# Attention outputs moved to the middle of a slot, their copies to its end, in a top-k attention and mixture-of-experts kernel

## Chip, cores and metric

The kernel runs on one core of a Trainium2 chip. The metric is the device time of one execution in microseconds (us), lower is better. The core's engines are called by the short names of the profile: PE (TensorE: matmuls and transposes; PEld is its weight load), DVE (VectorE), ACT (ScalarE), POOL (GpSimd) and SP (SyncE, which issues transfers).

## What is computed

Two blocks follow each other. The first is attention with a top-k mask: 8 batches, 8 heads, 576 tokens, head size 64; every row of scores keeps its 32 largest values. The second is a mixture of experts without dropping: 4608 tokens of 512 numbers, 8 experts with a hidden size of 1024, and each token goes to the one expert with the highest logit.

```python
scores = scale * np.matmul(q, k.transpose(0, 1, 3, 2))
kth = np.partition(scores, -top_k, axis=-1)[..., -top_k:-top_k + 1]
scores = np.where(scores >= kth, scores, -1000000000.0)
attn = np.exp(scores - np.max(scores, axis=-1, keepdims=True))
attn = attn / (np.sum(attn, axis=-1, keepdims=True) + 1e-09)
attn_out = np.matmul(attn, v)
x = attn_out.transpose(0, 2, 1, 3).reshape(B * S, H * D)
...
logits = x @ w_gate
expert_idx = np.argmax(logits, axis=1)
...
h = np.maximum(x_sorted[lo:hi] @ w1[e], 0.0)
y_sorted[lo:hi] = h @ w2[e]
...
return (gate_w[:, None] * y)
```

## The kernel before

The attention works on *units*: a unit is one batch and one pair of heads, so there are four units to a batch. Two units are worked off together, an even and an odd one. For each such pair the function groups gives nine *slots*; a slot is two tiles of 128 queries by 576 keys. Slots 0 to 3 of the nine are the four full tiles of the even unit, slot 4 has the 64 remaining queries of both units, and slots 5 to 8 are the full tiles of the odd unit. Eight batches with two pairs each make 144 slots. They are numbered through from 0 here, so slot i has the place i modulo 9.

All engines' queues for this stage are written out by hand in loop: the order in which the Python code calls the engines is the order of each engine's queue. One turn of the loop is one slot, and its work is spread over neighbouring turns:

- multiply makes the products of queries and keys (tile sc, L304, on PE) four slots ahead. They go to a pool of score banks in PSUM.
- scores copies them out (tile s, L311, on ACT) three slots ahead.
- search (L379, L390, L356, L320, L321, L327, L335, on DVE) finds the 32 largest values of each row in four rounds of eight. Each round takes one maximum per tile (L379), and the first three also strike the found values out (L390). The fold of the next slot's scores (L320, L321) stands ahead of the rounds, and fold_on (L327, and L335 for the tile hl) stands behind round two or ahead of round four. hl can also be made on POOL (L332, L333).
- When the search ends, ACT takes the threshold (tile low, L401), makes depths (L417) from it, POOL subtracts (less, L426), and ACT takes the exponentials (weights, L434), which leave their sums in z.
- transposed turns the exponentials of the slot before: PE transposes into wTm (L445, two banks), ACT copies them to wT (L452, or L450 in the slots with remaining queries), then PE transposes the rest to wTl (L461, L459) and ACT copies it to wTt (L469, L467).

The banks wTm, wTl, po and px come from one pool with the tag "t" that has two buffers, which are handed out in turn. A matmul into a bank waits until the copy out of the bank's last user is done.

When a unit's last full tile has been opened (place 3 for an even unit, place 8 for an odd one), loop starts ending for it. ending is a generator: it yields the name of the place in the loop at which it wants to go on, and at_place lets those go on that wait for the place it names. Through outputs it makes, step by step, po (weights times values, L482, two halves), its copies oT (L484, ACT), then px (L493, PE, turned back and multiplied by the gate), and the copies xl (L500, ACT). Between the two halves it calls divisors: ACT writes the sums plus epsilon to rz (L504, and L506, L507 or L509), and DVE takes the reciprocal (L511). The reciprocal is put on the list aside; tick takes one step from that list after each maximum and each strike of round three and four of a search, unless the slot is marked heavy. After that, logits (L519 to L524) and rows (L533) run on POOL and use xl and the reciprocal. The last unit of a batch then chooses the experts, ranks the tokens (ranks, places) and scatters them to the rows of their experts.

Expert blocks fill PE's time between. A block has 16 pieces (a piece of the first half is L979, one of the second L996), and pieces runs as many as a credit allows: a rate that the function level gives, times a share that depends on the slot's place. evacuate lets ACT copy out what a block has finished (xTs L870, hT L984, y L1005). In the last batch KEEP pieces are kept back, so that PE has work while the last unit's rows are sorted; after that the remaining blocks run.

The places of one turn of loop stand in this order before the change: the search (with "rows" beside it on POOL where the slot is heavy), "small", depths, less, "pool" (from slot 66 on also "relu" and "rows"), scores, "relu" (up to slot 65), evacuate, "turn", the wTm step, pieces, the wTl step, pieces, weights, the wTt copy, evacuate, multiply, the start of ending, "products", "weights", pieces.

Of the kernel before, what the change touches and what calls it, by code (L numbers as in the profile page):

```python
# [44 lines left out]
def kernel(  # L45
# [47 lines left out]
    nc = tc.nc  # L93
    B, U, P, _ = qk.shape
# [5 lines left out]
    NC = 4  # L100
    SM = NC * P
    ST = S - SM
    KC = NC + 1
# [4 lines left out]
    NT = 2 * NC + 1  # L108
# [25 lines left out]
    k = SimpleNamespace()  # L134
# [76 lines left out]
    for n in range(2):  # L211
        t = const.tile([P, S if n else KC * P], F32, name=f"oT{n}")
# [3 lines left out]
        t = const.tile([P, NT + 1], F32, name=f"rz{n}")  # L216
# [254 lines left out]
    def outputs(n, x):  # L471

        odd = n.u % 2
        oT = oT_of[odd]
        for j in range(2):
            q = slice(j * HF + (0 if odd else ST), (j + 1) * HF + (0 if odd else ST))
            po = bank("po")
            for c in range(KC):
                for h in range(2):
                    r = slice(h * D, (h + 1) * D)  # L480
                    rhs = wT[:, c, h, q] if c < NC else wTt[:, q]
                    nc.tensor.matmul(po[r, 0:HF], n.v[:, c, r], rhs, start=(c == 0), stop=(c == KC - 1))  # L482
            yield
            nc.scalar.copy(oT[:, j * HF:(j + 1) * HF], po[:, 0:HF])  # L484
            yield
        starts = [t * P + (ST if odd else 0) for t in range(NC)] + [0 if odd else SM]
        xw = P + lw
        n.xl = k.small.tile([P, KC, xw], F32, name="xl", bufs=1)
        put = []
        for t0, t1 in ((0, KC - 2), (KC - 2, KC)):  # L490
            px = bank("px")
            for t in range(t0, t1):
                nc.tensor.matmul(  # L493
                    px[:, (t - t0) * xw:(t - t0 + 1) * xw], oT[:, starts[t]:starts[t] + P],
                    turn[:, n.u // 2, odd * lw:odd * lw + xw], start=True, stop=True,
                )
            put.append((n.xl[:, t0:t1, :], px[:, 0:(t1 - t0) * xw].rearrange("p (t w) -> p t w", w=xw)))
        yield
        for to, px in put:
            nc.scalar.copy(to, px)  # L500

    def divisors(n):
        rz = rz_of[n.u % 2]
# [378 lines left out]
    def evacuate(upto=None):  # L882

        while due and (upto is None or upto in [kind for kind, _ in due]):
            due.pop(0)[1]()
# [127 lines left out]
            evacuate()  # L1013

    PIECES = 2 * FT
    FIRST = 13
    ARRIVED = 13
    AHEAD = 3
    QUIET = 66
    ON_CHIP = 3  # L1020
# [3 lines left out]
    with fast:  # L1024
# [86 lines left out]
        def ending(b, u):  # L1111

            nonlocal left
            n = unit[b * U + u]
# [22 lines left out]
            next(out_steps)  # L1137
            yield "relu"
            next(out_steps, None)
            yield "rows"  # L1140
            through(div)
            logits(n, lg)
# [7 lines left out]
            yield "turn"  # L1150
            through(r.steps)
            nc.scalar.activation(lg, lg, AF.Exp)
            yield "products"
            ranks(r)
            yield "small"
            steps = places(r, x)
            aside.append(steps)
            yield "relu"
            nc.scalar.copy(run, r.run)
            if b:  # L1160
                nc.scalar.activation(blocks, r.run, AF.Copy, scale=1.0 / P, bias=UNDER)
# [45 lines left out]
        late = []  # L1207

        def at_place(name):
            for end in list(late):  # L1210
                if end[1] == name:
                    end[1] = next(end[0], None)
                    if end[1] is None:
                        late.remove(end)
# [18 lines left out]
        def loop():  # L1233
# [16 lines left out]
            for i, (b, g) in enumerate(work):  # L1250
                tiles = tiles_of(i)
                u, tile = g[0]
                if tile == 0 and u % 2 == 0:
                    open_unit(tiles[0][0])
                if tails(tiles):
                    open_unit(tiles[1][0])

                loose = 0 < i < QUIET
                k.heavy = loose and "rows" in [place for _, place in late]
                soon = loose and (k.heavy or not k.crowded)  # L1260
                then = behind = beside = lambda: None
                if i + 1 < len(work):
                    def behind():
                        f_of[i + 1] = fold(s_of[i + 1])

                    then = lambda: fold_on(f_of[i + 1], soon and not k.heavy)
                    if i:
                        behind()
                        behind = lambda: None
                if k.heavy:  # L1270
                    beside = lambda: at_place("rows")
                held = k.heavy and k.crowded
                low, nbias, doubts = search(tiles, s_of[i], f_of.pop(i), then, soon, behind, beside)
                k.crowded, k.heavy = held, False
                at_place("small")
                w_of[i] = depths(s_of[i], low)
                less(s_of.pop(i), w_of[i])
                doubts()
                at_place("pool")
                if not loose:  # L1280
                    at_place("relu")
                    at_place("rows")
                put_stores()
                scatter(1)
                at = i % per_batch
                if at == FIRST and b:
                    rate = level(b) * PIECES / (U * NT)
                credit += rate * len(g)
                room = left
                if b == B - 1 and at >= ARRIVED:  # L1290
                    room -= KEEP
                    credit = room / (len(work) - i)
                share = {0: 0.5, 1: 1.2, 2: 1.6, 3: 0.5, 2 * NC: 1.4}[tile]
                now = max(0, min(int(credit * share + 0.5), room))
                credit -= now
                clock = i
                if i + AHEAD < len(work):
                    s_of[i + AHEAD], steps = scores(got_of.pop(i + AHEAD))
                    for step in steps:
                        step()  # L1300
                if loose:
                    at_place("relu")
                evacuate()
                at_place("turn")
                turns = turning(i - 1) if i else iter(())
                next(turns, None)
                part = min(BETWEEN, now - now // 2)
                rest = pieces(part)
                next(turns, None)
                rest = pieces(now - now // 2 - part + rest)  # L1310
                weights(tiles, w_of[i], nbias)
                next(turns, None)
                evacuate()
                if i + AHEAD + 1 < len(work):
                    multiply(i + AHEAD + 1)
                if tile == NC - 1:
                    end = ending(b, u)
                    late.append([end, next(end)])
                at_place("products")
                at_place("weights")  # L1320
                credit = min(credit + pieces(now // 2 + rest), 6 * rate)

            k.between = True
            for _ in turning(len(work) - 1):
                pieces(1)
            assert len(late) == 1
            clock = None
            for place in late[0][0]:
# [145 lines left out]
```

## Time and profile before

The time is the median of three runs. The profile is of one further execution.

| what | value |
| --- | --- |
| median of 3 runs | 1282.63 us (1281.47 to 1285.32) |
| the profiled execution: its own time | 1284.61 us |
| the profiled execution: its span | 1283.0 us |
| PE busy | 1176.1 us, 92% of the span |
| DVE busy | 1058.8 us, 83% |
| ACT busy | 933.3 us, 73% |
| POOL busy | 732.0 us, 57% |
| mean granted clock of TensorE | 0.967 |
| oT copies (L484) on ACT | 64, mean 399 ns |
| xl copies (L500) on ACT | 64, mean 463 ns |
| divisors (L504) on ACT | 32, mean 211 ns |
| reciprocals (L511) on DVE | 32, mean 207 ns |
| hl on DVE (L335) and on POOL (L332) | 107 and 37 |

The page is read from the slices of the span: they show which engine is full in which stage, and the shares over the whole span hide that the attention and the blocks behind it have different limits. A group of instructions is a line of the kernel, an engine, an operation and a tile, with the idle time of the engine just before it and what ended that idle time. Matmuls are pipelined and their ends modelled, so PE's busy time is a rough measure.

### The profile page before, as it was taken

How to read it: one execution, taken by the hardware profiler on the slowest of the kernel's cores; microseconds unless marked ns; L12 is line 12 of the kernel's file. 1: busy time of each engine (PE TensorE's matmuls, PEld its weight loads, DVE VectorE, ACT ScalarE, POOL GpSimd, SP SyncE). 2: the span in 40 equal slices, each digit the busy share in tenths (PEclk: the TensorE clock that was granted, in tenths of full speed). 3: DMA queues.
4: the chain of work that ended last, by engine and by line, in shares of the span. 5: the costliest groups of instructions: out<-in, count | busy, mean ns of one | idle time of the engine just before them, and what ended most of it. 6: DMA issues, size and time to landing. Idle time of an engine off the chain costs nothing. (4 is left out here: it accounts for less than half of the span.)

```text
span 1283.0 us, 24461 instructions
## 1 busy us (share of the span) xinstructions
PE 1176.1 (92%) x7574; PEld 823.6 (64%) x7574; DVE 1058.8 (83%) x4608; ACT 933.3 (73%) x2136; POOL 732.0 (57%) x884
## 2 busy tenths in 40 slices
PE   6767767898899999999999999999999999999998
PEld 3444444665566566667666666666666667789975
DVE  8999999999999999999999999999999965000000
ACT  4888887988799888888788888888888872112121
POOL 4777777786678665658555855676557743101010
PEclk9888788999899999999999999999999999999999
DMA  5001113741474147533946464547555548996582
GB/s 153 31 30 31 31 39 126 263 157 39 146 251 162 39 150 283 182 135 98 332 142 218 163 224 153 189 146 264 178 178 202 172 149 285 353 358 235 215 301 83
DMA packets 98701, 220.81 MB, mean 172 GB/s; under 512 B 5309, under 2 KB 26301, under 8 KB 98560
## 3 DMA queue, kind: packets, MB, share of 16 engines
q1 hardware_dynamic: 91360, 198.87, 44.5%
q0 software_dynamic: 6384, 19.97, 4.2%
q8 instruction: 61, 1.00, 0.3%
q14 instruction: 80, 0.66, 0.2%
q10 hardware_dynamic: 816, 0.31, 0.1%
HBM read 195.75 MB, written 24.04 MB: 171 GB/s over the span
## 5 line engine op out<-in xcount | busy, mean ns | idle before, releaser
L426 POOL TENSOR_TENSOR w<-s,w 128x576 f32<-128x576 f32 x288 | 409.2, 1441 | 317.5 <-ACT w L417 317.4
L979 PE MATMUL ph<-xTs,w 128*128 128x128 f32 x2112 | 263.0, 278 | 2.6 <-ACT xTs L870 2.6
L979 PEld LDWEIGHTS ph<-xTs,w 128*128 128x128 f32 x2112 | 251.3, 194 | 21.1 <-issue 17.6
L996 PE MATMUL py<-w,hT 128*128 128x512 f32 x528 | 248.7, 600 | 1.9 <-ACT hT L984 1.6
L434 ACT ACTIVATE w<-w,nbias 128x576 f32<-128x576 f32 x288 | 223.0, 785 | 2.3 <-POOL w L426 1.4
L445 PE MATMUL wTm<-turn,w 128*128 128x128 f32 x1152 | 173.9, 291 | 52.7 <-ACT oT L484 29.1
L417 ACT ACTIVATE w<-s,low 128x576 f32<-128x576 f32 x288 | 207.7, 768 | 4.7
L304 PE MATMUL sc<-qkb 64*128 64x288 f32 (+1 forms) x1280 | 200.7, 465 | 7.8 <-DMA qkb<-in_qk_dram 4.0
L445 PEld LDWEIGHTS wTm<-turn,w 128*128 128x128 f32 x1152 | 135.1, 148 | 111.6 <-ACT oT L484 35.5
L311 ACT COPY s<-sc 128x576 f32<-128x576 f32 x288 | 168.0, 634 | 11.9 <-PE sc L304 11.8
L379 DVE MAX8 tops<-scr 128x8 f32<-128x168 f32 x576 | 169.5, 328 | 0.0
L452 ACT COPY wT<-wTm 128x512 f32<-128x512 f32 x256 | 140.7, 596 | 37.8 <-PE wTm L445 37.2
L379 DVE MAX8 tops<-few 128x8 f32<-128x144 f32 (+1 forms) x576 | 154.9, 314 | 0.0
L304 PEld LDWEIGHTS sc<-qkb 64*128 64x128 f32 (+1 forms) x1280 | 107.1, 190 | 71.5 <-issue 35.2
L996 PEld LDWEIGHTS py<-w,hT 128*128 128x128 f32 x528 | 92.0, 191 | 86.5 <-issue 83.0
L482 PE MATMUL po<-wT,vb 128*64 128x288 f32 x1024 | 143.8, 425 | 0.0
L888 POOL DMA_INDIRECT out_dram<-y,xg x37 | 38.9, 1052 | 161.3 <-ACT y L1005 82.0
L356 DVE MAX8 few<-l 128x8 f32<-128x288 f32 x288 | 129.8, 451 | 0.0
L320 DVE TENSOR_TENSOR h<-s 128x576 f32<-128x576 f32 (+1 forms) x145 | 111.7, 770 | 3.9 <-ACT s L311 3.6
L321 DVE TENSOR_TENSOR l<-s 128x576 f32<-128x576 f32 (+1 forms) x145 | 114.3, 788 | 0.0
L482 PEld LDWEIGHTS po<-wT,vb 128*64 128x64 f32 x1024 | 70.1, 141 | 68.9 <-issue 17.4
L356 DVE MAX8 few<-hl 128x8 f32<-128x72 f32 x576 | 102.3, 221 | 0.0
(205 smaller groups left out, 1596.7 us busy)
## 6 DMA issues: line engine op xcount, KB each, us to landing
w<-in_moe_w_dram SPq DMA_DIRECT2D x74, 2048.0 KB, 9.2
qkb<-in_qk_dram SPq DMA_DIRECT2D x31, 608.0 KB, 3.8
vb<-in_v_dram SPq DMA_DIRECT2D x32, 320.0 KB, 3.2
xg<-x_rows SPq DMA_DIRECT2D x37, 257.0 KB, 9.1
x_rows<-blank SPq DMA_DIRECT2D x13, 257.0 KB, 7.9
x_rows<-blank POOLq DMA_DIRECT2D x4, 257.0 KB, 9.8
x_rows<-x,posi POOLq DMA_INDIRECT x40, 3.2
out_dram<-y,xg POOLq DMA_INDIRECT x37, 3.9
```

What stands on the lines that cost most here:

```text
L304: nc.tensor.matmul(ps[rows, j, 0:HF], n.q[d, cols], n.k[d, keys], start=True, stop=True)
L311: lambda m=m, ps=ps: nc.scalar.copy(s[:, m, :, :], ps[:, :, 0:HF]) for m, ps in enumerate(got)
L356: nc.vector.max(out=f.few[:, m, QF + 8 * j:QF + 8 * j + 8], in_=away)
L379: nc.vector.max(out=tops[:, m, r * 8:(r + 1) * 8], in_=src[m])
L417: nc.scalar.activation(w[:, m, :], s[:, m, :, :].rearrange("p j k -> p (j k)"), AF.Relu, scale=-STEEP, bias=low[:, m:m + 1],)
L426: k.last_pool = in_turn(nc.gpsimd.tensor_tensor(w[:, m, :], s[:, m, :, :].rearrange("p j k -> p (j k)"), w[:, m, :], op=ALU.subtract)).ins
L434: nc.scalar.activation(w[:, m, :], w[:, m, :], AF.Exp, scale=scale, bias=nbias[:, m:m + 1], accum_out=n.z[:, c:c + 1])
L445: nc.tensor.transpose(pm[:, c * P:(c + 1) * P], w[:, m, first:first + P], ident)
L452: nc.scalar.copy(wT[:, :, m, q], pm4)
L482: nc.tensor.matmul(po[r, 0:HF], n.v[:, c, r], rhs, start=(c == 0), stop=(c == KC - 1))
L979: nc.tensor.matmul(ph[:, f, :], n.w1[:, 0, dt, fc * P:(fc + 1) * P], n.xT[:, dt, :], start=(dt == 0), stop=(dt == DT - 1),)
L996: nc.tensor.matmul(py, hT[:, f, :], n.w2[:, 0, f, :], start=(f == 0), stop=(f == FT - 1))
```

## The change

In outputs the copies of px follow each half of px rather than both, with a step in between, so px takes two slots. In ending the second half of px and its copy are steps of their own ("products", "relu"), and rows come after a further place. In loop the place "products" moves from the end of the turn to its middle, between the wTm and the wTl step, and multiply moves along, behind it; the place "relu", at which the copies and the divisors are issued, moves from behind the score copies to behind the wTt copy. New places "ranks" and "early" keep the ranking and the copy of its counts where "products" and "relu" were. Rows run beside the search in all slots. FIRST and ARRIVED, the places at which a new batch's blocks enter the credit, go from 13 to 14, and the shares of pieces are given for each of the nine places.

```diff
     def outputs(n, x):
...
-        put = []
         for t0, t1 in ((0, KC - 2), (KC - 2, KC)):
             px = bank("px")
...
-            put.append((n.xl[:, t0:t1, :], px[:, 0:(t1 - t0) * xw].rearrange("p (t w) -> p t w", w=xw)))
-        yield
-        for to, px in put:
-            nc.scalar.copy(to, px)
+            yield
+            nc.scalar.copy(n.xl[:, t0:t1, :], px[:, 0:(t1 - t0) * xw].rearrange("p (t w) -> p t w", w=xw))
+            if t1 < KC:
+                yield
...
-    FIRST = 13
-    ARRIVED = 13
+    FIRST = 14
+    ARRIVED = 14
+    SHARES = (0.5, 0.5, 1.05, 1.6, 0.5, 1.6, 0.55, 1.1, 1.6)
...
             next(out_steps, None)
+            yield "products"
+            next(out_steps)
+            yield "relu"
+            next(out_steps, None)
+            yield "weights"
             yield "rows"
...
-            yield "products"
+            yield "ranks"
             ranks(r)
...
-            yield "relu"
+            yield "early"
             nc.scalar.copy(run, r.run)
...
-                k.heavy = loose and "rows" in [place for _, place in late]
-                soon = loose and (k.heavy or not k.crowded)
+                k.heavy = "rows" in [place for _, place in late]
+                soon = k.heavy or loose and not k.crowded
...
                 at_place("pool")
-                if not loose:
-                    at_place("relu")
-                    at_place("rows")
                 put_stores()
...
-                share = {0: 0.5, 1: 1.2, 2: 1.6, 3: 0.5, 2 * NC: 1.4}[tile]
+                share = SHARES[i % NT]
...
-                if loose:
-                    at_place("relu")
+                at_place("early")
                 evacuate()
                 at_place("turn")
                 turns = turning(i - 1) if i else iter(())
                 next(turns, None)
                 part = min(BETWEEN, now - now // 2)
                 rest = pieces(part)
+                at_place("products")
+                if i + AHEAD + 1 < len(work):
+                    multiply(i + AHEAD + 1)
                 next(turns, None)
                 rest = pieces(now - now // 2 - part + rest)
                 weights(tiles, w_of[i], nbias)
                 next(turns, None)
+                at_place("relu")
                 evacuate()
-                if i + AHEAD + 1 < len(work):
-                    multiply(i + AHEAD + 1)
                 if tile == NC - 1:
                     end = ending(b, u)
                     late.append([end, next(end)])
-                at_place("products")
+                at_place("ranks")
                 at_place("weights")
...
             for _ in turning(len(work) - 1):
                 pieces(1)
+            at_place("rows")
```

## The prediction

> **What bounds the kernel now.** I read the page's slices (part 2) first, then the busy time by stages, the waits of PE, and last the timeline of one slot. Each digit of the slices is a tenth of busy time in 32 us:
>
> ```profile
> PE   6767767898899999999999999999999999999998
> DVE  8999999999999999999999999999999965000000
> PEclk9888788999899999999999999999999999999999
> ```
>
> VectorE stands at 9 from the second slice until the attention ends, near 1047 us; after that PE alone is full. The busy time by stages (columns: stage, length, then busy us of PE, PE's weight loads, DVE, ACT, POOL, then clock and DMA) sharpens it:
>
> ```profile
> 20.00:100.00 80.00, 57.45 (x320) 35.20 (x320) 80.00 (x353) 67.82 (x156) 62.33 (x77) 0.85 0.10 33
> 100.00:500.00 400.00, 339.66 (x2185) 224.58 (x2185) 399.76 (x1762) 342.25 (x795) 291.48 (x351) 0.93 0.38 133
> 600.00:1000.00 400.00, 393.04 (x2640) 269.94 (x2642) 398.08 (x1697) 341.36 (x791) 247.36 (x291) 1.00 0.56 197
> ```
>
> VectorE is never idle: 399.76 of 400 us, then 398.08. So each of the 144 slots lasts as long as its VectorE work (6.55 us with hl on GpSimd, 6.9 to 7.1 without, more where sums for the routing ride along), and what makes VectorE wait lengthens the attention by as much. Behind it about 235 us of expert blocks follow on PE (1047 to 1283), a fixed number of them. PE's waits from 500 to 1047 us, and then from 20 to 500 us:
>
> ```profile
> PE wTl L461 <- ACT wT L452: 5.2, 11, 1.1
> ...
> PE wTm L445 <- ACT xl L500: 0.9, 1, 0.9
> ```
>
> ```profile
> PE wTm L445 <- ACT oT L484: 29.1, 21, 3.5
> PE wTl L461 <- ACT wT L452: 21.0, 20, 3.1
> PE wTm L445 <- ACT xl L500: 16.4, 6, 3.4
> ```
>
> PE's waits for the oT and xl copies, 45.5 us, lie before 500 us, where PE has room and VectorE sets the pace. Removing them there buys nothing by itself.
>
> One slot in which an odd unit makes its divisors (timeline, start and length in us):
>
> ```profile
> 77.46 0.20 ACT L401 ACTIVATE low<-tops 128x2 f32<-128x2 f32 x1 [1.16 <-DVE tops L379]
> ...
> 80.09 0.41 ACT L484 COPY oT<-po 128x288 f32<-128x288 f32 x1
> ...
> 80.38 0.23 ACT L504 ACTIVATE rz<-z 128x9 f32<-128x9 f32 x1
> 80.49 0.20 ACT L506 ACTIVATE rz<-z 64x1 f32<-64x1 f32 x1
> ...
> 80.72 0.20 ACT L507 ACTIVATE rz<-z 64x1 f32<-64x1 f32 x1
> 80.82 1.04 ACT L452 COPY wT<-wTm 128x512 f32<-128x512 f32 x2
> ...
> 82.57 0.21 DVE L511 RECIPROCAL rz<-rz 128x10 f32<-128x10 f32 x1
> ...
> 83.42 0.24 ACT L469 COPY wTt<-wTl 128x128 f32<-128x128 f32 x1
> ```
>
> The search of slot 9 ends when low starts. VectorE goes straight into search 10, and 5.11 us later reaches the reciprocal of this unit's divisors, which ScalarE wrote 1.65 us before. That margin is what the change spends.
>
> **What the Trainium skill says.** *PSUM — Partial Sum Buffer*, "Engine vs sequencer instructions": the queues of ScalarE, VectorE and GpSimd are strict FIFO, and matmuls start and end in program order. The timeline agrees: the search went on only behind the reciprocal. *TensorE: Matmul & The Clock Gate*, "What's actually happening": the array's clock is throttled unless recent activity releases it. The stages agree: clock 0.85 where PE is 72% busy, 1.00 where it is 98%. *SBUF — State Buffer*, "Who interferes with whom": a VectorE operation with two SBUF inputs contends with GpSimd's reads. Moving rows (L533, 1253 to 1804 ns) may thus cost VectorE some tenths; I take 0.
>
> **The change, part by part.** Times below count from low.
>
> *Divisors.* They go from behind the score copies to the end of ScalarE's queue for the slot, behind the exponentials, wTt and oT. In the built program's order the reciprocal stays where it was, in the next search behind the first of the two maxima of round three (due at 5.11; from slot 66 on, where fold_on comes in the last round, at about 4.77). It waits for the last divisor. Behind it in VectorE's queue stands the whole rest of the search, and all engines wait for that.
>
> *Even units* (slots 5, 14, ...): with nothing in front of the exponentials wTt starts at 5.12 (so in slots 1, 3, 8 of before). Two wTt copies (pitch 0.25) and two divisors (0.2 each) end at 6.02. Stall: 6.02 + 0.05 (a release) - 5.11 = 0.96 early, 1.3 late, plus ScalarE's lag from the slot before.
>
> *Odd units* (slots 9, 18, ...): here po is made in the same slot, now ahead of sc and wTl. Its bank is that of the first wTm, so po waits for the first wT copy, which ends at 3.23 where nothing stands ahead. Then 20 matmuls (2.58 to the next start), sc (1.17) and wTl (0.27), with two releases of 0.05: wTt starts at 7.35 instead of 5.12, oT at 7.60, the divisors at 7.89 (0.29 later), and the last ends at 8.43. Stall: 8.43 + 0.05 - 5.11 = 3.4 early, 3.7 late. In seven of the odd units (slots 27, 45, ... 135) the built program has the reciprocal one search or more later, behind routing sums: no stall there.
>
> *Lag.* A slot with po (four in nine) now takes ScalarE until 7.60 + 0.41 = 8.0, against 6.6 to 7.0 of VectorE: a lag of some 1.2. A slot with px ends near 5.9 and wins 1.0 back. So an even unit's slot begins 1.2 to 1.4 late, and about 1.2 more behind an odd unit without stall (two po slots in a row, nothing reset). An odd unit's begins about 0.2 late. Copies for expert blocks ahead of the wT copies (0.5 each, in most late po slots, few early) add 0.4 late.
>
> *Sum of stalls.* Up to slot 65: four odd x 3.6 = 14.4, five even x 2.2 = 11, two even behind an unstalled odd x 3.3 = 6.6: 32. From 66: four odd x 4.1 = 16.4, four even x 2.9 = 11.6, five even x 4.2 = 21: 49. Together 81 us.
>
> *Clock and PE's order.* With the attention longer PE is idle more, and its clock falls. Between nothing and 20 us: at 0.85 the 4 us of po, sc and wTl grow by 0.7, and 24 stalls by some 0.85. I take 6, since early the pace hardly changes and late PE stays near nine tenths.
>
> *The rest.* hl goes from VectorE to GpSimd in one slot: -0.5. rows in every slot stand between nbias and less on GpSimd; 2.6 us of logits and rows end before less is due, so 0 (up to 0.5 a unit if xl comes late). px in two slots, sc earlier, the shares: the same matmuls, 385 pieces ahead of the last wTm against 384. In the tail po of the last unit moves behind the last wTm (2.6 us), but PE has kept blocks there and the sum of its work stays: 0 to 2.6, I take 1. SP's issues of q, k, v loads follow sc and po by part of a slot; their use is slots away: 0.
>
> Sum against the profiled execution (span 1283.0, its own time 1284.61): 1284.6 + 81 + 6 - 0.5 + 1 = 1372. The median of the runs, 1282.63, is 2 us lower, inside what I can tell.
>
> **Rivals.**
> *Short stalls:* po does not hold up wTl (PE early enough, or the lag is caught up), so only ScalarE's queue counts. Even 0.96 x 7 + 1.3 x 9 = 18, odd 1.15 x 4 + 1.5 x 4 = 11, expert copies 5: 34, so 1319. For: ScalarE's busy share is 85% in both halves. Against: po's bank and the order po, sc, wTl are fixed.
> *Long stalls:* PE cools to 0.85 everywhere (+20) and, with idle gaps of 1.7 us ahead of po in four slots and 0.7 in the others (10 us in nine), exceeds its room late: 64 us of work + 10 against 72, +1.7 for eight and a half pairs, 14. 1284.6 + 81 + 34 = 1400. Against: a late PE has no such gaps.
> *Faster:* the freed PE time counts and the reciprocal is not late. It decides if the divisors end before 5.1 us; then PE's late wait for xl (0.9), VectorE's idle time in the two long stages (2.2) and hl's 0.5 go: 1281. Against: even with an empty queue wTt alone ends past 5.1.
> *No effect:* gains elsewhere, or cover, cancel the stalls: 1283. Nothing in the stages offers 40 us.
>
> **How the numbers follow.** Forecast 0.6, short 0.2, long 0.12, faster 0.05, no effect 0.03. A difference of 0.3%, 4 us, is what can be told from none; so faster 0.05, same 0.03, slower 0.92. The likeliest case reaches from 1345 to 1395; with most of the other two slow ones the range is 1316 to 1402.
>
> **What would show it.** VectorE waits at the reciprocal (L510) for ScalarE's divisors (L505, L506, L508) some 24 times, 2 to 4.5 us each, 60 to 100 us in all, and VectorE's busy time stays near 1058. PE's waits for oT ahead of wTm shrink to the ends of slots; wTt waits for wTl in po slots. If VectorE shows no such wait, the argument is wrong at its root; if it waits about 1 us each, the po, sc, wTl step failed.

## The result and the profile after

The kernel after the change takes 1467.3 us (median of four runs, 1464.37 to 1470.44), the kernel before 1283.67 us on the same chip: a ratio of 1.1423, 95% interval 1.1403 to 1.1442. The change makes the kernel 184 us slower. The forecast was 88 us slower, with an upper end of 1402: the sign was right, the size was not.

The slices of the span after the change (a slice is now 37 us):

```profile
PE   7666666788888888988988889898889888999998
DVE  8888789978998999798987997889989994400000
PEclk9977777799999999999999999999999999999999
```

VectorE no longer stands at 9 through the attention, and the PE clock is at 7 for six slices early on. The busy time by stages, with the columns of the table shown before (PE, weight loads, DVE, ACT, POOL, clock, DMA):

```profile
20.00:100.00 80.00, 54.46 (x256) 32.76 (x256) 68.08 (x294) 55.54 (x128) 50.69 (x63) 0.89 0.09 28
100.00:500.00 400.00, 304.53 (x1762) 192.73 (x1762) 358.46 (x1456) 285.40 (x663) 250.49 (x297) 0.85 0.29 100
600.00:1000.00 400.00, 350.75 (x2215) 236.21 (x2216) 355.53 (x1443) 290.64 (x674) 202.93 (x245) 0.96 0.46 158
```

VectorE is idle 41.5 of 400 us in the second stage and 44.5 in the third, where it was idle 0.2 and 1.9. The counts in brackets tell more: 1456 and 1443 VectorE instructions fit into stages that held 1762 and 1697. The busy share fell by a tenth, the work done by a sixth, so the instructions got longer as well. The groups of VectorE show both (columns: busy us and mean ns, then idle time just before and what ended it), first in the kernel before, then after the change:

```profile
L327 DVE TENSOR_TENSOR few<-h 128x288 f32<-128x288 f32 x144 | 80.2, 557 | 0.0
L335 DVE TENSOR_TENSOR hl<-h 128x288 f32<-128x288 f32 x107 | 51.1, 477 | 0.0
L511 DVE RECIPROCAL rz<-rz 128x10 f32<-128x10 f32 x32 | 6.6, 207 | 7.2 <-ACT rz L507 5.7 <-ACT rz L509 1.6
```

```profile
L327 DVE TENSOR_TENSOR few<-h 128x288 f32<-128x288 f32 x144 | 95.6, 664 | 0.0
L335 DVE TENSOR_TENSOR hl<-h 128x288 f32<-128x288 f32 x106 | 74.2, 700 | 0.0
L510 DVE RECIPROCAL rz<-rz 128x10 f32<-128x10 f32 x32 | 6.7, 209 | 112.4 <-ACT rz L508 60.7 <-ACT rz L506 51.7
```

The reciprocal waited 7.2 us in all before, 5.7 of them behind the last unit. Now it waits 112.4 us, for the two kinds of last divisors. The waits over all engines (us in total, times, longest) name the next ones:

```profile
ACT wTt L469 <- PE wTl L461: 231.2, 117, 5.5
...
PE po L482 <- ACT wT L452: 88.5, 43, 4.6
POOL xl L518 <- ACT xl L497: 83.9, 31, 8.6
...
DVE h L320 <- POOL hl L332: 15.0, 10, 2.7
...
DVE h L320 <- ACT s L311: 6.7, 6, 3.0
```

PE's waits for the oT and xl copies between 20 and 500 us, 45.5 us before, have gone. In their place PE waits for wT ahead of po, ScalarE for wTl, and GpSimd for xl (11.7 us before, once).

From the two traces the attention, taken from the end of the first search to the end of the last, divides like this. VectorE is the engine that sets it, so its own busy time and its waits make up the whole:

| us | before | after | difference |
| --- | --- | --- | --- |
| VectorE's own time | 1026.7 | 1089.8 | +63.1 |
| its wait at the reciprocal | 1.6 | 105.4 | +103.8 |
| its wait at h, for s or hl | 0.6 | 18.8 | +18.2 |
| its other waits | 0.6 | 0.5 | -0.1 |
| attention | 1029.5 | 1214.5 | +185.0 |
| from there to the end of the span | 235.5 | 236.7 | +1.2 |

Slot 9, whose timeline stands in the prediction for the kernel before, now reads (start and length in us; in brackets the idle time before and what ended it):

```profile
86.55 0.22 ACT L401 ACTIVATE low<-tops 128x2 f32<-128x2 f32 x1
...
89.20 1.08 ACT L452 COPY wT<-wTm 128x512 f32<-128x512 f32 x2
89.85 3.58 PE L482 MATMUL po<-wT,vb 128*64 128x288 f32 x16 [2.07 <-ACT wT L452]
90.02 0.80 DVE L327 TENSOR_TENSOR few<-h 128x288 f32<-128x288 f32 x1
...
93.21 0.97 PE L482 MATMUL po<-wTt,vb 128*64 128x288 f32 x4
94.11 1.20 PE L304 MATMUL sc<-qkb 64*64 64x288 f32 x16
95.25 0.33 PE L461 MATMUL wTl<-turn,w 128*128 128x128 f32 x1
95.61 0.27 ACT L469 COPY wTt<-wTl 128x128 f32<-128x128 f32 x1 [2.63 <-PE wTl L461]
95.77 0.40 ACT L484 COPY oT<-po 128x288 f32<-128x288 f32 x1
96.39 0.20 ACT L506 ACTIVATE rz<-z 64x1 f32<-64x1 f32 x1
96.63 0.22 DVE L510 RECIPROCAL rz<-rz 128x10 f32<-128x10 f32 x1 [4.96 <-ACT rz L506]
```

This is the chain that the prediction laid out: wT copy, po, sc, wTl, wTt, oT, divisors, reciprocal. The reciprocal could have run at 96.63 - 4.96 = 91.67, which is 5.12 us after low (forecast 5.11). po starts 3.30 after low, on the release of its bank (forecast 3.28). But from po to sc there are 94.11 - 89.85 = 4.26 us, where the forecast had 2.58 from the kernel before. So wTt starts 9.06 after low rather than 7.35, and the wait is 4.96 rather than 3.4. PE had been idle for 2.07 us ahead of po.

### The profile page after: what moved, and what is told of

The parts are those of the page before. It is cut to its first block, busy times and chain, and to the rows that moved or that the text cites. A ratio compares the mean times of both kernels' runs of the same rounds, so it can differ in the third digit from the quotient of the medians.

```text
span 1468.8 us, 24561 instructions
## 1 busy us (share of the span) xinstructions
PE 1242.5 (85%) x7574; PEld 853.3 (58%) x7574; DVE 1122.2 (76%) x4607; ACT 933.1 (64%) x2136; POOL 731.5 (50%) x886
## 5 line engine op out<-in xcount | busy, mean ns | idle before, releaser
L978 PE MATMUL ph<-xTs,w 128*128 128x128 f32 x2112 | 255.8, 276 | 4.9 <-ACT xTs L869 3.5
L482 PE MATMUL po<-wT,vb 128*64 128x288 f32 x1024 | 179.2, 505 | 89.4 <-ACT wT L452 88.5
L304 PE MATMUL sc<-qkb 64*128 64x288 f32 (+1 forms) x1280 | 214.5, 472 | 21.7 <-ACT s L311 18.1
L445 PE MATMUL wTm<-turn,w 128*128 128x128 f32 x1152 | 165.0, 288 | 43.8 <-ACT wTt L469 22.9
L469 ACT COPY wTt<-wTl 128x128 f32<-128x128 f32 x128 | 34.1, 266 | 232.1 <-PE wTl L461 231.2
L482 PEld LDWEIGHTS po<-wT,vb 128*64 128x64 f32 x1024 | 82.0, 165 | 168.1 <-ACT wT L452 107.3
L304 PEld LDWEIGHTS sc<-qkb 64*128 64x128 f32 (+1 forms) x1280 | 116.5, 196 | 96.2 <-issue 35.5
L995 PEld LDWEIGHTS py<-w,hT 128*128 128x128 f32 x528 | 97.4, 198 | 91.5 <-issue 85.9
L321 DVE TENSOR_TENSOR l<-s 128x576 f32<-128x576 f32 (+1 forms) x145 | 117.8, 813 | 0.0
```

Of the source, the lines that this page charges most:

```text
L304: nc.tensor.matmul(ps[rows, j, 0:HF], n.q[d, cols], n.k[d, keys], start=True, stop=True)
L445: nc.tensor.transpose(pm[:, c * P:(c + 1) * P], w[:, m, first:first + P], ident)
L978: nc.tensor.matmul(ph[:, f, :], n.w1[:, 0, dt, fc * P:(fc + 1) * P], n.xT[:, dt, :], start=(dt == 0), stop=(dt == DT - 1),)
L995: nc.tensor.matmul(py, hT[:, f, :], n.w2[:, 0, f, :], start=(f == 0), stop=(f == FT - 1))
```

## The experiments

Three theories stood at the start. The expectations call them A: the late divisors stall VectorE, as predicted, and that alone is the loss. B: ScalarE's lag behind VectorE, which comes from wTl standing behind po and sc, is the deeper cause; it makes less late on GpSimd, and so VectorE's two-input operations longer, whether or not a reciprocal waits. C: rows and logits come before xl is there, and GpSimd is held up by that. Later runs add the shares of pieces, the idle and cold PE, the copies at the slot's end, and po and px in the middle (called G); each says in words what it tests. "Own time" below is VectorE's in the attention, as in the table above, and each ratio is against the kernel before, run beside it.

**The divisors early again, in the kernel after.**

```diff
+            div = divisors(n)
+            if u % 2:
+                yield "early"
+                next(div)
+                aside.append(div)
             yield "products"
...
             if u % 2 == 0:
+                yield "early"
+                next(div)
+                aside.append(div)
                 yield "relu"
-            div = divisors(n)
-            next(div)
-            aside.append(div)
```

> The changed kernel with the divisors issued where they stood before (behind the score copies, early in ScalarE's slot); po, sc, wTl and the copies stay as changed. Theory A (the reciprocal's wait for late divisors is the loss, all else follows from it): the waits at the reciprocal, 104 us in the attention, go, and with them most of the rest: 1290 to 1320 us. Theory B (po ahead of wTl makes ScalarE late in every slot with po; the reciprocal is only where VectorE first meets it): the reciprocal's waits go, but ScalarE's lag is no longer reset there and comes back as waits for the score copies (h <- s) and as VectorE operations made longer beside GpSimd: 1350 to 1420 us.

1397.75 us, ratio 1.0873 (1.0854 to 1.0891): 70 us better than after. The groups of VectorE in this run:

```profile
L327 DVE TENSOR_TENSOR few<-h 128x288 f32<-128x288 f32 x144 | 108.0, 750 | 0.0
L335 DVE TENSOR_TENSOR hl<-h 128x288 f32<-128x288 f32 x106 | 76.4, 721 | 0.0
L510 DVE RECIPROCAL rz<-rz 128x10 f32<-128x10 f32 x32 | 6.4, 201 | 19.4 <-ACT rz L508 12.5 <-ACT rz L506 6.8
```

The wait at the reciprocal falls by 93 us, yet few and hl get longer, not shorter: own time is 1115.9, 89 above before, and 15.7 us of waits at h remain. Without the stalls VectorE runs further ahead of ScalarE: the mean lag of low behind the end of its search is 1.95 us up to slot 65 and 2.44 from there, against 1.7 and 2.09 in the kernel after. So A is a cause, but not the only one, and the time lies in the band of B.

**wTl ahead of po and sc, in the kernel after.**

```diff
                 rest = pieces(part)
+                next(turns, None)
                 at_place("products")
                 if i + AHEAD + 1 < len(work):
                     multiply(i + AHEAD + 1)
-                next(turns, None)
```

> The changed kernel with wTl made before po or px and sc; the divisors stay at the end of the slot. Theory A: every reciprocal still waits for divisors behind the exponentials and wTt, about 1 to 1.5 us in 24 slots plus a small lag: 30 to 60 us of waits, 1320 to 1345 us. Theory B: with wTt in time ScalarE has no lag, and the waits shrink to under 30 us: 1285 to 1315 us.

1374.05 us, 1.0722 (1.0669 to 1.0775): 93 us better, and outside the bands of both theories. Still 24 reciprocals wait, 71.9 us in all, but own time falls to 1045.6, the waits at h to 2.0 us, and the mean lag to 0.51 and 0.89. By this measure the order po, sc, wTl costs more than the late divisors do, though the two can't be added up: a third of what this edit gains lies in the waits at the reciprocal (105.4 to 71.9).

**Both together.**

> Both edits: divisors early and wTl before po. Theories A and B: no waits at the reciprocal, no lag, VectorE's operations as long as before: 1278 to 1292 us. Theory C (rows beside the search, too early for the xl copies, hold up GpSimd, and less, and so ScalarE): GpSimd's waits for xl stay near 80 us, and 15 to 40 us of the loss remain: 1300 to 1325 us.

1331.72 us, 1.0364 (1.0347 to 1.0382): 136 us better than after, less than the sum 70 + 93, as each takes part of the same waits. Reciprocals wait 7.6 us. 47 us remain, more than either band allowed, 39.4 of them own time (1066.1). The wait of ScalarE that leads in this run (from its waits):

```profile
ACT oT L484 <- PE po L482: 84.7, 61, 4.2
```

With the divisors out of the way the oT copy at the slot's end waits for po, in 61 of 64 cases. Whether it costs anything is seen further down, where the copies go back.

**Only the divisors late, in the kernel before.**

```diff
             if u % 2 == 0:
                 yield "relu"
+            yield "ends"
             div = divisors(n)
...
                 next(turns, None)
+                at_place("ends")
                 evacuate()
```

> The kernel before with one edit: the divisors are issued at the end of ScalarE's slot, behind the wTt copy; everything else as before. Theory A: the reciprocals in the next search wait about 1 us early and 1.5 to 3 us late (ScalarE's lag of before comes on top) in some 24 slots: 30 to 60 us of waits, 1315 to 1345 us. Theory B: without po ahead of wTl the divisors are nearly in time: under 15 us, 1283 to 1298 us.

1333.56 us, 1.0381 (1.0363 to 1.0398). Its groups of VectorE:

```profile
L327 DVE TENSOR_TENSOR few<-h 128x288 f32<-128x288 f32 x144 | 73.0, 507 | 0.0
L511 DVE RECIPROCAL rz<-rz 128x10 f32<-128x10 f32 x32 | 6.9, 216 | 67.6 <-ACT rz L509 38.6 <-ACT rz L507 27.7 <-ACT rz L506 1.3
```

This one edit turns the kernel before into one whose reciprocals wait: 61.6 us in the attention, as A had it. The time grows by only 49, since own time falls by 12: a stalled VectorE lets ScalarE catch up (the mean lag of low behind the search's end falls from 0.24 to 0.23 us up to slot 65, and from 1.32 to 0.43 from slot 66 on), and few goes from 557 to 507 ns. In the change the lag grew at the same time, and this discount turned into a surcharge.

**Logits and rows one slot later, in the kernel after, and on top of both edits.**

```diff
             next(out_steps, None)
             yield "weights"
+            yield "weights"
             yield "rows"
...
+            at_place("weights")
             at_place("rows")
```

> The changed kernel with logits and rows one slot later alone. Theory C: GpSimd's 84 us of waits for xl go, and with them part of the lag: 1410 to 1440 us. Theory B (po ahead of wTl makes the lag): ScalarE stays as late, under 15 us less: 1452 to 1470 us.

> Divisors early, wTl before po, and logits and rows one slot later (one further place), so that GpSimd does not reach them before the last xl copy. Theory C (GpSimd's waits for xl, 48 us with both edits, delay less, and less then lies beside VectorE's fold_on and hl): the waits go to under 10 us, few<-h and hl fall by 15 to 25 us of the 25 they are above before, 1305 to 1315 us. Rival (the lag comes from ScalarE's waits for po at the end of the slot, 85 us, not from rows): 1325 to 1332 us.

Alone 1431.54 us, 1.1162 (1.1128 to 1.1195), 36 us better than after; on top of both edits 1325.6, 1.033 (1.0305 to 1.0356), only 6 better than without.

The first time lies in the band of C, but not for the reason that C gives. GpSimd's waits for xl do go, from 83.9 us to 9.9, yet VectorE's own time rises from 1089.8 to 1102.3 us, and the mean lag rises to 2.34 us up to slot 65 and 3.06 after it. What falls are the waits at the reciprocal, from 105.4 to 35.3 us. The edit moved the reciprocals too: a search with rows beside it takes no step from aside, so with rows one slot later 22 of the 32 reciprocals come one search later, by which time their divisors have long been written. On top of both edits, where reciprocals hardly wait, the waits for xl fall from 47.6 to 9.9 us and 6 us are gained. More than these 6 us are not shown for theory C.

**Rows beside the search in all slots, in the kernel before.**

```diff
-                k.heavy = loose and "rows" in [place for _, place in late]
-                soon = loose and (k.heavy or not k.crowded)
+                k.heavy = "rows" in [place for _, place in late]
+                soon = k.heavy or loose and not k.crowded
...
-                if not loose:
-                    at_place("relu")
-                    at_place("rows")
...
-                if loose:
-                    at_place("relu")
+                at_place("relu")
```

> The kernel before with one part of the change alone: from slot 66 on the copies and divisors stay behind the score copies, and rows run beside the next search as they do before slot 66. Theory: here xl is copied early in the slot before, GpSimd does not wait, so within 8 us of before, 1276 to 1292 us. Theory C in its strong form (2.6 us of GpSimd work ahead of less costs in itself): 1295 to 1310 us.

1289.07 us, 1.0042 (1.0028 to 1.0056): this part alone costs 5 us.

**The shares and FIRST and ARRIVED, one way and the other.** Into the kernel before the new ones; into the kernel after, and into the version with both edits and later rows, the old shares back.

```diff
-                share = {0: 0.5, 1: 1.2, 2: 1.6, 3: 0.5, 2 * NC: 1.4}[tile]
+                share = SHARES[i % NT]
```

> The kernel before with the new shares of pieces and the entry of a batch's blocks one slot later. If the spread of pieces has a part in the loss: 1290 to 1310 us. If not: within 6 us of before, 1278 to 1290 us.

> The changed kernel with the old shares of pieces alone put back. If the new shares are a loss of their own (as in the kernel before, +52 us): 1405 to 1430 us. If they only suit the new order, in which the slots with po have little room: the same or worse, 1460 to 1500 us.

> Divisors early, wTl before po, rows one slot later, and the old shares. If the shares are a loss of their own, most of the remaining 42 us go: 1280 to 1298 us. If they suit the order: 1325 to 1350 us, from more pieces ahead of ScalarE's waits for po at the end of the slot.

In the kernel before the new shares cost 52 us (1336.02, 1.0402, 1.0375 to 1.0429), far above both bands. In the kernel after they are worth 12: with the old ones it takes 1479.63 (1.1511, 1.1492 to 1.1531), and the other version 1337.61 (1.0417, 1.0391 to 1.0442) against 1325.6. The shares belong to their order: each set is the better one where it was used.

**PE kept busy, in the kernel after:** three matmuls whose result nobody uses, in slots 1 to 23.

```diff
                 rest = pieces(part)
+                if 0 < i < 24:
+                    warm = k.ps_m.tile([P, Dm], F32, name="warm", tag="m")
+                    for _ in range(3):
+                        nc.tensor.matmul(warm, ident, blank[:, 0:Dm], start=True, stop=True)
```

> The changed kernel with idle PE time filled: in slots 1 to 23, where no expert block runs, three more matmuls of 128x512 into a free bank between the wTm step and po (their result is not used). Theory D (PE's clock falls in the gaps, po takes 4 to 5 us for 2.65, and the stalls grow by it): po is back near 2.65 in these slots, the six waits at the reciprocal there shrink by 1 to 2 us each and the slots with po by the lag: 8 to 25 us less, 1442 to 1459 us. If PE's clock has no part: no gain, 1465 to 1475 us.

1451.13 us, 1.1278 (1.1248 to 1.1308): more work, 16 us less time. Its slot 9, timeline, where low starts at 80.29:

```profile
83.57 2.16 PE L482 MATMUL po<-wT,vb 128*64 128x288 f32 x16 [0.71 <-ACT wT L452]
84.21 1.55 DVE L327 TENSOR_TENSOR few<-h 128x288 f32<-128x288 f32 x1
85.56 0.66 PE L482 MATMUL po<-wTt,vb 128*64 128x288 f32 x4
...
87.64 0.27 ACT L469 COPY wTt<-wTl 128x128 f32<-128x128 f32 x1 [1.29 <-PE wTl L461]
...
88.66 0.22 DVE L510 RECIPROCAL rz<-rz 128x10 f32<-128x10 f32 x1 [2.04 <-ACT rz L506]
```

po is as fast as in the kernel before again, with a granted clock of 1.00 from 80 to 90 us, where the kernel after has 0.78 from 86 to 96. wTt starts 87.64 - 80.29 = 7.35 after low, the forecast's figure to the hundredth. So the 1.7 us that slot 9 was late came from the slower PE. The same lines show the other loss: few takes 1.55 us, so VectorE reaches the reciprocal more than 1 us later, at 88.66 - 2.04 = 86.62, or 6.33 after low, and waits the less for it. In this slot a part of the loss moves from "wait" to "own time"; over the whole attention own time stays (1089.0) and the waits at the reciprocal fall to 92.8 us.

**Where the rest of both edits lies.** With divisors early and wTl first, the copies go back behind the score copies; from there, sc goes back to the slot's end, or po and px do; the last run has the second of these with the old shares.

```diff
                         step()
+                at_place("relu")
                 at_place("early")
...
                 next(turns, None)
-                at_place("relu")
                 evacuate()
+                at_place("products")
```

(The last line belongs to the run with po and px at the slot's end, where "products" is taken out of the middle; for sc it is the call of multiply that goes.)

> Divisors early, wTl before po, and the copies of po and px put back behind the next slot's score copies (rows follow one slot later with them): po, px and sc in the middle of the slot and the new shares are what is left of the change. Theory E (the 42 us left with both edits come from ScalarE waiting for po at the end of its slot, 85 to 91 us, which makes it late and lays less beside VectorE's fold_on): ScalarE's wait for po goes under 30 us, few<-h and hl are back within 5 us of before, 1278 to 1296 us. Rival (sc and po in the middle of the slot, or the shares, are a loss of their own): 1305 to 1335 us.

> Divisors, wTl and the copies as before, sc back at the end of the slot; po and px in the middle and the new shares stay. Theory F (sc in the middle pushes the expert pieces and the next wTm together, or makes the score copies wait): 1280 to 1296 us. Theory G (po in the middle): still 1310 to 1330 us. Theory H (the shares are a loss wherever po stands): still 1310 to 1335 us.

> The same with sc in the middle and po and px back at the end of the slot, new shares. Theory F: still 1310 to 1330 us. Theory G: 1280 to 1296 us. Theory H: 1320 to 1340 us, as in the kernel before with the new shares (1336).

> Sc back at the end and the old shares; po and px stay in the middle. Theory H: 1276 to 1290 us, near or below before. Theories F and G: no better than the same kernel with the new shares.

Copies early: 1324.81 (1.0319, 1.0305 to 1.0333), 7 us better than both edits alone. Rows come one slot later with them, and later rows alone had given 1325.6, so the place of the copies is worth next to nothing here, although ScalarE's waits for po ahead of oT fall from 84.7 to 4.5 us. sc at the end besides: 1319.95 (1.0279, 1.0262 to 1.0296), 5 more. po and px at the end instead: 1291.79 (1.007, 1.0044 to 1.0096), 33 better, own time 1032.0. sc at the end with the old shares: 1374.4 (1.0704, 1.0684 to 1.0724), 54 worse than with the new, so the shares are not what holds the rest (theory H). ScalarE's waits with the copies early, and then with po and px at the slot's end:

```profile
ACT s L311 <- PE sc L304: 46.0, 55, 2.4
```

```profile
ACT s L311 <- PE sc L304: 7.3, 6, 2.2
```

With po and px in the middle the score copies wait for sc 55 times; with them at the end, 6 times, although sc stays in the middle. po and px there make PE late for its next matmuls and ScalarE after it. That is G, and with sc in the middle it holds most of the rest. It is not a price of po's place by itself: in the kernel before with the new shares, where sc, po and px all stand at the slot's end, the time was 1336.02. 7 us over the kernel before (1284.46 in these runs) remain; rows beside the search (5 when alone) are one candidate, and the sum was not taken apart further. No version was faster than the kernel before.

**GpSimd beside VectorE, in the kernel before.** The longer operations rested so far on comparing lengths. The traces show what goes with them. Two operations of the kernel after, the first GpSimd's less:

```profile
81.96 1.63 POOL L426 TENSOR_TENSOR w<-s,w 128x576 f32<-128x576 f32 x1
82.25 1.65 DVE L335 TENSOR_TENSOR hl<-h 128x288 f32<-128x288 f32 x1
```

hl starts while less runs, and ends 0.31 us after it. So it is with 75 of the 82 few and hl that start inside a less with over 0.15 us of it left; few then takes 1.00 us on average (57 times) and hl 1.51 (25), all others 0.45. In the kernel before only 24 few and 4 hl start so. To test the cause, useless work on GpSimd was put behind nbias from slot 66 on: a subtraction, or memsets, which read nothing, and then a subtraction that in_turn keeps at its place in the queue.

```diff
                 at_place("small")
+                if i >= QUIET and "rows" not in [place for _, place in late]:
+                    in_turn(nc.gpsimd.tensor_tensor(blank[:, 0:Dm], blank[:, 0:Dm], blank[:, 0:Dm], op=ALU.subtract))
                 w_of[i] = depths(s_of[i], low)
```

> The kernel before, with one useless subtraction (128x512, two inputs, about 1.3 us by less' 1.45 us for 576) on GpSimd in 37 of the 78 late slots, between nbias and less, where GpSimd is idle for 3.5 to 4.2 us. It lies beside VectorE's fold_on (few<-h and hl<-h, 0.46 us each there). If GpSimd's two-input work lengthens VectorE's two-input work as the lengths beside and alone in the changed kernel say (0.81 to 0.88 against 0.45 us), each of these slots gains 0.5 to 0.9 us of VectorE's own time: 18 to 33 us, the time goes to 1300 to 1315, and the waits at the reciprocal and at h stay below 5 us in sum. If the longer operations were a mark of late slots and not their cause, own time stays within 3 us and the time within 1282 to 1288.

> The same 37 slots and the same place on GpSimd, with three useless memsets of 128x512 (about 0.52 us each, 1.5 us together) in place of the subtraction: as long on GpSimd, but nothing is read. If what lengthens VectorE's two-input operations is GpSimd's reading beside them, this costs nothing: 1282 to 1288. If any work of GpSimd there costs (its queue, what it makes late), it costs as much as the subtraction: 1300 to 1315.

> The kernel before with the useless subtraction (128x512, 1.1 us) tied into GpSimd's queue in 77 of the 78 late slots, directly behind nbias and ahead of less, where GpSimd is idle for some 3.5 us; the order on all other engines is that of before. It lies beside VectorE's fold_on (few<-h and hl<-h, 0.46 us each) of these slots. If GpSimd's reading beside them lengthens VectorE's two-input operations as in the changed kernel (0.81 to 0.88 against 0.45 us), a slot gains 0.4 to 0.9 us of VectorE's own time: 30 to 65 us, the time goes to 1315 to 1350 with few and hl at 0.7 us and more in these slots and no new waits. If the long operations only mark late slots and aren't caused by GpSimd, own time and time stay: 1281 to 1289.

The first two missed their place. Without in_turn an instruction that depends on nothing doesn't keep it, and the useless ones were pulled ahead: they ran between 18 and 147 us (the subtractions) and 264 us (the memsets), where slot 66 begins at about 550. They took 1359.28 (1.058, 1.0559 to 1.0601) with the subtraction, 1366.05 (1.0634, 1.0611 to 1.0657) with memsets, most of it by VectorE's waits for hl from GpSimd, 55.5 and 61.7 us. Their expectations were also written for 37 slots where the condition holds in 77. So their times tell nothing of the question, but their traces do. First h beside a subtraction (in brackets VectorE's wait for hl):

```profile
76.73 1.03 POOL L1277 TENSOR_TENSOR blank<-blank 128x512 f32<-128x512 f32 x1
76.80 1.58 DVE L320 TENSOR_TENSOR h<-s 128x576 f32<-128x576 f32 x1 [8.02 <-POOL hl L332]
```

Then h beside a memset:

```profile
65.52 0.53 POOL L1278 MEMSET blank<- 128x512 f32 x1
65.62 0.76 DVE L320 TENSOR_TENSOR h<-s 128x576 f32<-128x576 f32 x1 [1.88 <-POOL hl L332]
```

h takes 1.58 us in 7 of the 8 cases in which it starts inside a useless subtraction, and 0.74 to 0.76 in all 20 in which it starts inside a memset; few takes 0.96 on average (8 times) and 0.44 (8 times). Alone they take 0.74 and 0.44. So it is GpSimd's subtraction that holds them up, not any work of GpSimd.

The third shows what that costs: 1311.01 us, 1.0206 (1.0182 to 1.023), with the order on VectorE, ScalarE and PE unchanged and no new waits of VectorE. Two of its slots, timeline:

```profile
1040.48 1.05 POOL L1277 TENSOR_TENSOR blank<-blank 128x512 f32<-128x512 f32 x1
1040.55 1.30 DVE L327 TENSOR_TENSOR few<-h 128x288 f32<-128x288 f32 x1
...
1048.16 1.03 POOL L1277 TENSOR_TENSOR blank<-blank 128x512 f32<-128x512 f32 x1
1049.53 0.44 DVE L327 TENSOR_TENSOR few<-h 128x288 f32<-128x288 f32 x1
```

Beside the subtraction few takes 1.30 us; 7 us later, when the subtraction has ended first, 0.44. Over all slots, few takes 1.27 us where over 0.1 us of it lies beside the subtraction (16 times) and h 1.22 (15 times); one more h, with five other operations of GpSimd beside it, took 5.1. Slots 66 to 143 get longer by 27.2 us, and all of that is own time: against the kernel before h adds 9.4 us, few 8.7, l 6.7, and small operations of the routing most of the rest. The time came out 4 us below the expected band because few and h were beside the subtraction only 32 times; in the second slot shown it ends 0.3 us before few starts. hl kept 0.45, against the expectation: in its ten cases hl starts 0.11 us first, and the subtraction gets longer instead, 1.23 us for 1.04.

## Why the prediction was right in kind and wrong in size

*The bound, and that the freed PE time is worth nothing:* right. PE's 45.5 us of waits for oT and xl went, and the attention got no shorter for it.

*The mechanism of the stalls:* right. VectorE waits at the reciprocal for the divisors at L506 and L508, 24 times in the attention, as counted, 1.1 to 8.0 us each, and the seven odd units that were named as safe don't wait. The rivals with shorter stalls, with no effect and with a faster kernel fell by this. The kernel before with late divisors alone shows that the step does it by itself. *PSUM — Partial Sum Buffer*, "Engine vs sequencer instructions", in the Trainium skill (queues strictly in order) carried this step, and the run agrees: the search stands still at the reciprocal for 4.96 us in slot 9.

*The sum of stalls:* too small. By the prediction's own terms, with the waits of the profile:

| units | forecast | measured |
| --- | --- | --- |
| up to slot 65: four odd | 14.4 | 20.0 |
| five even | 11 | 13.8 |
| two even behind an unstalled odd | 6.6 | 6.5 |
| from slot 66: four odd | 16.4 | 24.7 |
| four even | 11.6 | 15.7 |
| five even behind an unstalled odd | 21 | 24.7 |
| sum | 81 (and 6 for the clock) | 105.4 |

The sum for an odd unit (wT copy, po, sc, wTl) was right where PE was busy enough: 7.35 with the added matmuls. The clock was mis-sized: "I take 6". A block of po took 3.39 us on average against 2.73 before, over 3 us in 26 of 64 cases (16 of 28 up to slot 65) against 4. Filling PE's idle time in slots 1 to 23 alone gave 16 us back. *TensorE: Matmul & The Clock Gate*, "What's actually happening", says that a PE which has been idle is throttled; the trace agrees in kind (clock 0.85 from 100 to 500 us), while the prediction took "early the pace hardly changes" as a reason for a small price, where early is just where PE is idle. The rival with the long stalls had priced a cooler PE at 20.

*"\*SBUF — State Buffer\*, Who interferes with whom ... I take 0":* the failed step. The section says that an operation of VectorE with two inputs contends with GpSimd's reads, and the prediction applied it to rows, which moved, and not to less, which did not move in the queue but came later in time, since it waits for ScalarE. A less that comes late meets few and hl, which then end only behind it. The prediction took VectorE's work as fixed ("VectorE's busy time stays near 1058"); it rose to 1122.2. In the attention own time grew by 63.1 us, a third of the loss: hl +23.8, few +16.6, l +4.4, and the rest in small operations of the routing, of which 48 now start inside a less and take 0.63 us on average (25 before); the others take 0.18. The runs agree with the section in that subtractions of GpSimd hold VectorE up and memsets don't, and they give the size: an operation of 0.45 us ends 0.31 us behind the less that it meets.

*Lag:* "some 1.2", and about 1.2 more behind an odd unit without stall. Measured, the lag went up to 9 us in single slots and averaged 1.7 up to slot 65 and 2.1 after it, from 0.24 and 1.32. The prediction used the lag only to lengthen stalls. It did not ask who else waits for ScalarE: s and hl reach VectorE late (18.2 us at h, not in the forecast), and less comes late on GpSimd.

*logits and rows, "0 (up to 0.5 a unit if xl comes late)":* the condition came true, as xl was late 31 times, 83.9 us of waiting on GpSimd. The bound, 16 us for 32 units, is not contradicted: with both edits, later rows take away most of those waits and gain 6 us.

*Shares, "the same matmuls":* true of the count and beside the point. With one order the new shares cost 52 us, with the other they bring 12. Zero missed by 12 us here only because these shares were paired with this order; that was luck.

*Tail:* forecast 1, measured 1.2: right. *Range:* it took its upper end from stalls and clock alone. Own time (63) and the waits at h (18) on top of 1372 give 1453, and the stalls at their measured size (104 more than before instead of 81 + 6) 1470, which is what the profiled execution took (1470.44).

## What to carry to other kernels

When instructions move to the end of an in-order queue, find their first reader on the engine that is full and compare the two times within one slot; here the divisors were 1.65 us early (3.46 us after low) and moved to 6.0 us by the forecast's count in even units, 8.4 in odd ones. Then follow the lag itself, not only the wait: every operation that hangs on the late engine slides in time without moving in its queue, and what it slides beside has a price. When an edit that delays one thing makes a kernel faster, see what else it moved: the later rows moved 22 reciprocals, and the trace puts the gain at their waits. A tuned split of filler work belongs to one order of issue and is tested together with it.

## What the runs showed of the hardware that was not expected

A maximum or minimum of two inputs on VectorE that starts while GpSimd subtracts doesn't slow down by a share: in nearly all cases (75 of 82 few and hl of the kernel after) it ends a fixed time after the subtraction, 0.31 to 0.33 us for 128x288 and 0.61 to 0.63 for 128x576, which take 0.44 and 0.74 us alone. Beside a memset on GpSimd both keep their length. When VectorE starts first, it is GpSimd's subtraction that gets longer, 1.23 us for 1.04 in ten cases. And useless matmuls can shorten a kernel: a block of 20 matmuls that took 4.26 us from its start to the next matmul after 2.07 us of idle PE took 2.57 us after 0.71 us of it, and the whole kernel became 16 us faster with 69 matmuls more.
